# Block sums of w1 from DRAM scratch, and 512-column block products in three passes of a token-mixing MLP kernel

## The chip, the cores and the metric

The kernel runs on one NeuronCore of a Trainium2 chip. The core has TensorE (PE in the profile, with its weight loads listed apart as PEld), VectorE (DVE), ScalarE (ACT) and GpSimd (POOL), and SyncE (SP), which here only issues transfers. Sixteen DMA engines carry the transfers that SP, ACT and POOL issue. Each engine works through its own queue in order and waits on semaphores for the others. Matrix products accumulate in PSUM, which the kernel's pools divide into banks of 128 x 512 float32. The metric is the time of one execution on the device in microseconds (us), the median over the runs.

## The reference

One sequence of S = 2048 tokens with D = 512 channels, all float32. First an attention block with a learned feature map in 32 heads, then a token-mixing MLP with F = 1792 hidden units:

```python
qkv = _layernorm(x) @ wqkv                      # split into q, k, v, 32 heads of 16
phi = concat([softmax(q @ w_phi), softmax(-q @ w_phi)])      # the same for k
kv  = einsum("bhsf,bhsd->bhfd", phi_k, v);  z = phi_k summed over s
h   = x + (phi_q @ kv / (phi_q . z + 1e-6)) @ wo
n   = _layernorm(_layernorm(h))
u   = gelu(einsum("bsd,sf->bdf", n, w1) + b1)   # (512, 1792): tokens are contracted
y   = einsum("bdf,fs->bds", u, w2) + b2
out = h + y transposed
```

The change touches the first product of the MLP, `n` with `w1` (2048 x 1792). That is the reference's longest product together with the one with `w2`.

## The kernel before, in words

**Precision.** Every float32 operand is split into a high part of reduced precision (`hi`, made by a ScalarE copy) and the remainder (`lo`, made by a subtraction on VectorE or POOL). A product is three matmuls: hi x hi, hi x lo, lo x hi. `mm3` (lines 71 to 73) issues these; the third is the first that needs the lo part of its stationary operand. `split` (lines 66 and 67) makes the two parts.

**Stages.** The first stage (up to about 130 us) loads x in 16 tiles of 128 tokens, splits each (`split_x`: hi on ScalarE, lo on POOL) and computes k, v and q logits from it. `k_step(t)` multiplies tile t by the k weights, normalises the keys of tile t - 1 (`k_norm`, on VectorE and POOL), and loads and splits tile t + 2 into one of three raw buffers. The sums over tokens of keys and values (`kv`) are formed for four tiles at a time; the first four follow the v product of tile 4. In this stage the order of TensorE's work is written out by hand. The queues of SP, POOL, VectorE and ScalarE are there ordered by the framework's scheduler, which simulates the program and puts an instruction where it becomes ready, so the order in the queue need not be the order of the code. From the middle of the kernel on (from `ms`, after the last k product) all five orders are those of the code.

A second stage (up to about 263 us) forms the attention output and h. The MLP follows.

**The products with w1.** Seven passes, each over 256 columns of w1 (p = 0 to 6) and all 2048 tokens. Passes 0 and 1 run beside the second stage. The others are named by `KINDS = "vuuuv"`: pass 2 and pass 6 are plain ("v"), passes 3, 4 and 5 are block passes ("u"). A pass has eight steps of 256 tokens; steps are numbered through, so passes 3, 4, 5 are steps 8 to 31. After them come the products with w2 ("y" steps, from `Y0` = 40).

A block step takes a 256 x 256 piece of w1 as a 2 x 2 array of blocks and, instead of eight block products, forms seven, from sums of blocks of both operands. The seven weight blocks of a step lie in places 0 to 6 of a raw tile: 1 to 4 are the blocks of w1 as loaded, 0, 5 and 6 are sums, and place 1 is overwritten with a sum at the end. `w_sums` (lines 793 to 805) makes these on VectorE for a pair of steps. `w_parts` (808 on) splits a step's seven blocks into hi and lo. `load_raw(g)` issues the loads of pair g on SP, into one of four pair places (two tiles of two pairs); `prepare` calls it as soon as both steps of the pair that had the place are split.

**The seven products.** `products` (line 1007) issues each of them with `narrow` (line 989): three matmuls over 256 columns (hi x hi, hi x lo, lo x hi), 21 per step. The other form, `wide` (lines 996 and 998), takes hi x (hi and lo together) over 512 columns into a whole bank and then lo x hi over 256 columns into the bank's first half, so that two matmuls and two weight loads do the work of three; the bank's halves are added afterwards. The y steps (`wide_step`) have four of the seven products in this form and three as `narrow`: 17 matmuls per step. The block passes do not use it.

**Banks.** A block pass before uses four banks: pass 4 those of `ps_b`, passes 3 and 5 those of `ps_f` and `ps_q`. So two passes in a row use different banks. `u_out` (with `firsts`) forms the four output pieces from them: one ScalarE copy and five VectorE operations, issued right after the pass's last step has been issued.

**Adding transfers.** A DMA issued from POOL can add into its destination. The kernel has this in three places: for sums of u (line 951), for some weight sums of the y steps (line 790) and for the output (line 1039). SP's transfers cannot add. Each transfer that is issued on SP or ACT takes one of eight semaphores in turn (`DMAHW0` to `7` in the listings below), and waits for the transfer that had it before.

Of the kernel before, what the change touches and what calls it, by code (L numbers as in the profile page):

```python
# [9 lines left out]
F32 = mybir.dt.float32  # L10
# [7 lines left out]
P = 128  # L18
# [15 lines left out]
PLAIN = 2  # L34
KINDS = "vuuuv"
HD = D // 2
# [6 lines left out]
def block_kernel(ctx: ExitStack, tc: tile.TileContext, x, xT, wT, phic, wo, w1, b1, w2, b2,  # L43
# [61 lines left out]
    kvp = ps_kv.tile([P, 4, 64], F32, name="kvp")  # L105

# [174 lines left out]
    with tc.tile_pool(name="prep", bufs=1) as prep:  # L281
# [511 lines left out]
    def w_sums(g):  # L793
# [3 lines left out]
        plain = STEPS[2 * g][0] == "y"  # L797
        raw = BLOCK[g // 2 % 2] if plain else RAW[g]
# [8 lines left out]
    def w_parts(n):  # L807
# [8 lines left out]
        split(PARTS[n][0][:, k], PARTS[n][1][:, k], RAW[n // 2][:, n % 2, k], nc.vector)  # L816
# [189 lines left out]
    def four_banks(i):  # L1006
        return [new_bank(q) for q in ((ps_b,) * 4, (ps_f, ps_f, ps_q, ps_q))[i]]
# [7 lines left out]
    def firsts(banks):  # L1015
        a, b, c, d = banks
        tmp = wqp.tile([P, 4, HD], F32, name="tmp", tag="small")
        nc.scalar.activation(tmp[:, 1], a[:, 0], AF.Copy)
        nc.vector.tensor_sub(tmp[:, 2], a[:, 1], tmp[:, 1])
        nc.vector.tensor_sub(tmp[:, 3], tmp[:, 2], d[:, 0])  # L1020
        nc.vector.scalar_tensor_tensor(tmp[:, 0], b[:, 0], -1.0, tmp[:, 2], op0=ALU.mult, op1=ALU.subtract)
        return tmp[:, 0:2], tmp[:, 3].unsqueeze(1).to_broadcast([P, 2, HD])

    def u_out(p, banks):
        e, u3 = firsts(banks)
        U[p] = o = ur.tile([P, 4, HD], F32, name="u")
        nc.vector.tensor_add(o[:, 0:2], banks[1], u3)
        nc.vector.tensor_add(o[:, 2:4], banks[2], e)
# [187 lines left out]
    def prepare(m):  # L1216
# [8 lines left out]
        elif m % 2 == 0 and m + 2 < Y0:  # L1225
            w_sums(m // 2 + 1)
# [27 lines left out]
def _layout(A_x, A_wqkv, A_w_phi, A_wo, B_w1, B_b1, B_w2, B_b2):  # L1254
# [7 lines left out]
    for a in range(P // DH):  # L1262
# [11 lines left out]
        "w1": np.asarray(B_w1),  # L1274
        "b1": np.asarray(B_b1).reshape(NF, P).T,
# [23 lines left out]
```

## Time and profile before

| | |
|---|---|
| median of 3 runs | 515.43 us (515.14 to 515.83) |
| profiled execution, first to last instruction (span) | 513.1 us |
| outside the span, against the median | 2.3 us |
| granted TensorE clock | 1.000 |
| TensorE busy | 507.8 us (99%) |
| weight loads busy | 441.7 us (86%) |
| VectorE, ScalarE, POOL busy | 438.4 (85%), 310.6 (61%), 261.1 (51%) us |
| block passes (steps 8 to 31) | 288.6 to 349.1 us |
| y steps | from 370.9 us |

The page gives the profiled execution by its span; its own device time is not listed apart from the three runs, so it is held against their median here. A row of the page's groups names line, engine, operation, output and inputs; a row of a timeline begins with start and duration. A row of the chain has start, duration and what ran. In a row of the waits stand who waited, for whom, the total in us, how often, and the longest. In a row by windows, each engine's busy time stands with its number of instructions, and at the end the granted clock, the busy share of the DMA engines and GB/s. "To landing" is the time from issue to the transfer's completion. Matmuls overlap, so the duration of one (0.28 or 0.39 us) is longer than the distance to the next, which is what counts.

### The profile page before, as it was taken

Reading aid. Unit: us, or ns where it says so; the run is one execution under the profiler, and the core shown is the slowest. Engines: PE = TensorE matmul, PEld = TensorE weight load, DVE = VectorE, ACT = ScalarE, POOL = GpSimd, SP = SyncE. Lnnn points to the kernel's source line nnn. Section 1 sums busy time; section 2 is a strip of 40 time slices with the busy share of each in tenths; the row PEclk is TensorE's granted clock in tenths of the full one; section 3 lists DMA queues with packets and bytes.
Section 4 is the critical chain, followed back from the end, with each engine's and each line's share of the span. In section 5 each row is a group of like instructions: output and inputs, shape, how many; then the busy total and the mean of one; then the engine's idle time right before and its main releaser. Section 6 shows DMA issues by size and latency. Waiting matters only on the chain.

```text
span 513.1 us, 10496 instructions
## 1 busy us (share of the span) xinstructions
PE 507.8 (99%) x4024; PEld 441.7 (86%) x4024; DVE 438.4 (85%) x746; ACT 310.6 (61%) x557; POOL 261.1 (51%) x212
## 2 busy tenths in 40 slices
PE   8999999999999999999999999999999999999997
PEld 8888888888877777777788999998899999999997
DVE  6799889989887899699877898898799889868983
ACT  6999863525267878867676754577655444434530
POOL 3579997876999999985200421202323212211220
PEclk9999999999999999999999999999999999999999
DMA  8642301010123234354325775545677797668734
GB/s 308 217 144 84 103 22 42 1 65 21 42 64 103 67 100 145 127 169 132 95 69 185 150 159 125 133 115 151 173 164 147 181 199 167 122 153 190 169 51 85
DMA packets 53266, 63.35 MB, mean 123 GB/s; under 512 B 4832, under 2 KB 39904, under 8 KB 53216
## 3 DMA queue, kind: packets, MB, share of 16 engines
q1 hardware_dynamic: 44288, 51.90, 32.5%
q0 software_dynamic: 8640, 10.62, 14.9%
q8 instruction: 31, 0.51, 0.4%
q10 hardware_dynamic: 288, 0.17, 0.1%
q14 instruction: 19, 0.16, 0.1%
HBM read 48.39 MB, written 11.14 MB: 116 GB/s over the span
## 4 chain that ended last, share of the span: by engine, by line
PE 95%; DVE 2%; ACT 1%; DMA 1%; issue 0%; POOL 0%; DVEq 0%
PE py L989 25%; PE py L996 9%; PE pu L71 9%; PE pu L72 8%; PE pu L73 8%; PE py L998 4%; PE pk_ps L71 3%; PE pk_ps L72 3%; PE pk_ps L73 3%; PE pv L73 3%; PE pv L71 3%; PE pv L72 3%; PE po L71 3%; PE po L73 2%; PE po L72 2%; PE pn L616 2%
## 5 line engine op out<-in xcount | busy, mean ns | idle before, releaser
L66 ACT ACTIVATE wp<-wraw 128x896 fp32r<-128x896 f32 (+1 forms) x96 | 82.4, 895 | 68.3 <-DVE wraw L805 23.9
L67 DVE TENSOR_TENSOR wp<-wraw,wp 128x896 fp32r<-128x896 f32 (+1 forms) x96 | 95.5, 1019 | 14.9 <-ACT wp L66 14.6
L989 PE MATMUL py<-cb,wp 128*128 128x256 f32 x678 | 92.6, 283 | 0.0
L989 PEld LDWEIGHTS py<-cb,wp 128*128 128x128 f32 x678 | 86.1, 191 | 0.0
L1039 POOL DMA_DIRECT2D out<-u x28 | 24.8, 963 | 89.8 <-ACT u L1085 28.9
L951 POOL DMA_DIRECT2D tt<-u x14 | 13.4, 960 | 60.6 <-ACT tt L950 34.5
L490 POOL TENSOR_TENSOR ez<-eq,zB 128x1024 f32<-128x1024 f32 x16 | 38.4, 2406 | 3.8 <-ACT zB L550 3.8
L219 POOL TENSOR_TENSOR pk<-pk,sk 128x1024 f32<-128x1024 f32 x16 | 31.1, 1947 | 11.3 <-DVE sk L218 10.1
L996 PE MATMUL py<-cb,wp 128*128 128x512 f32 x126 | 36.1, 394 | 0.0
L514 POOL TENSOR_TENSOR eq<-eq,w 128x1024 f32<-128x1024 f32 x16 | 32.4, 2025 | 3.5 <-DVE w L511 3.5
L223 POOL TENSOR_TENSOR zacc<-zacc,pk 128x1024 f32<-128x1024 f32 x13 | 31.4, 2412 | 0.5
L989 PE MATMUL py<-hs,wp 128*128 128x256 f32 x216 | 30.0, 283 | 0.0
L989 PEld LDWEIGHTS py<-hs,wp 128*128 128x128 f32 x216 | 27.8, 192 | 0.1
L195 ACT ACTIVATE pk<-pk,r 128x1024 f32<-128x1024 f32 x16 | 18.4, 1149 | 15.0 <-DVE pk L173 14.4
L989 PE MATMUL py<-uf,wp 128*128 128x256 f32 x198 | 26.6, 283 | 0.0
L71 PE MATMUL pu<-wq,xs 128*128 128x512 f32 x64 | 26.1, 409 | 0.0
L71 PE MATMUL pu<-hs,whl 128*128 128x512 f32 x64 | 26.0, 406 | 0.0
L71 PE MATMUL po<-woh,oh 128*128 128x512 f32 x64 | 25.3, 396 | 0.1
L72 PE MATMUL pu<-wq,xs 128*128 128x512 f32 x64 | 25.0, 391 | 0.0
L73 PE MATMUL pu<-wq,xs 128*128 128x512 f32 x64 | 25.0, 390 | 0.0
L72 PE MATMUL pu<-hs,whl 128*128 128x512 f32 x64 | 25.0, 390 | 0.0
L73 PE MATMUL po<-woh,ol 128*128 128x512 f32 x64 | 25.0, 390 | 0.0
(226 smaller groups left out, 1422.1 us busy)
## 6 DMA issues: line engine op xcount, KB each, us to landing
wraw<-in_w SPq DMA_DIRECT2D x112, 256.0 KB, 3.4
out<-u POOLq DMA_DIRECT2D x21, 256.0 KB, 5.4
xraw<-in_xT SPq DMA_DIRECT2D x16, 256.0 KB, 2.9
xh<-in_x SPq DMA_DIRECT2D x16, 256.0 KB, 2.7
h<-in_x SPq DMA_DIRECT2D x16, 256.0 KB, 2.9
out<-h SPq DMA_DIRECT2D x16, 256.0 KB, 2.0
wraw<-in_wT SPq DMA_DIRECT2D x12, 256.0 KB, 4.9
tt<-u POOLq DMA_DIRECT2D x14, 128.0 KB, 3.8
```

The source lines that it names most:

```text
L66: nc.scalar.activation(hi, src, AF.Copy)
L67: lo_engine.tensor_sub(lo, src, hi)
L71: nc.tensor.matmul(o, ah, bh, start=first, stop=False)
L72: nc.tensor.matmul(o, ah, bl, start=False, stop=False)
L73: return nc.tensor.matmul(o, al, bh, start=False, stop=last).ins
L219: nc.gpsimd.tensor_mul(heads(PK[t]), heads(PK[t]), sk.unsqueeze(2).to_broadcast([P, 2 * H, DH]))
L223: nc.gpsimd.tensor_add(zacc, zacc, PK[t])
L490: nc.gpsimd.tensor_mul(EZ[t], EQ[t], zB)
L514: nc.gpsimd.tensor_mul(heads(EQ[t]), heads(EQ[t]), W[t].rearrange("p g c h -> p (g c h)").unsqueeze(2).to_broadcast([P, 2 * H, DH]))
L989: nc.tensor.matmul(o, w[:, m[0]], x[:, y], start=opens and i == 0, stop=closes and i == 2, skip_group_check=True)
L996: nc.tensor.matmul(o, wh_[:, m[0]], x(m[1]), start=first, stop=False, skip_group_check=True)
L1039: nc.gpsimd.dma_start(out[t * P:(t + 1) * P, k * HD:], flat(a), accum_op=ALU.add)
```

## The change

Two of the four weight sums of a block step are no longer made on VectorE. They come from DRAM scratch (`ZS`, two tensors of 512 KB for each block pass). These are filled in the first stage: `sum_copy` copies one set of w1's blocks from DRAM to DRAM on SP, and `sum_add` adds another set into it with an adding transfer on POOL. There are six of each. The code calls them in `k_step` from t = 5 and from t = 9. For this the host passes w1's columns of the block passes a second time, in the order of the blocks (`w1u`).

`load_raw` of a block pair loads blocks 2 to 4 from `w1u` in one transfer and the two sums from the scratch in two. The raw tile of a pair is laid out block by block, with the two steps side by side. `w_sums` is called for two pairs at once and makes the remaining two sums of both in two operations of 512 elements.

The products of a block step use `wide` for four of the seven. A block pass has six banks: four of `ps_b` in all three passes, and two of `ps_q` or `ps_f` in turn. `u_out` has five ScalarE copies and nine VectorE operations.

```diff
@@ in block_kernel
+    def sum_copy(p, k):
+        nc.sync.dma_start(rows(ZS[p][k]), rows(w1u[US.index(p), (2, 0)[k]]))
+
+    def sum_add(p, k):
+        nc.gpsimd.dma_start(rows(ZS[p][k]), rows(w1u[US.index(p), k]), accum_op=ALU.add, max_dma_last_dim=8192)
@@ in k_step
             k_norm(t - 1)
+            if 5 <= t < 11:
+                sum_copy(US[(t - 5) // 2], (t - 5) % 2)
+            if 9 <= t < 15:
+                sum_add(US[(t - 9) // 2], (t - 9) % 2)
@@ in load_raw
+        kind, i, j = STEPS[2 * g]
+        if kind == "u":
+            RAW[g] = RAW[g].rearrange("p n m s -> p (n m s)").rearrange("p (m n s) -> p m n s", m=7, n=2)
+            cols = slice(j * P, j * P + 2 * P)
+            nc.sync.dma_start(RAW[g][:, 2:5].rearrange("p m n s -> p m (n s)"),
+                              w1u[US.index(i), 1:4, :, cols].rearrange("m p s -> p m s"))
+            for k in range(2):
+                nc.sync.dma_start(RAW[g][:, k].rearrange("p n s -> p (n s)"), ZS[i][k][:, cols])
+            return
@@ in w_sums
-        plain = STEPS[2 * g][0] == "y"
-        raw = BLOCK[g // 2 % 2] if plain else RAW[g]
+        raw = BLOCK[g // 2 % 2]
+        if STEPS[2 * g][0] == "u":
+            v = raw.rearrange("p (g n) m s -> p g (n m s)", g=2).rearrange("p g (m s) -> p g m s", m=7)
+            nc.vector.tensor_add(v[:, :, 5], v[:, :, 0], v[:, :, 2])
+            nc.vector.tensor_add(v[:, :, 6], v[:, :, 4], v[:, :, 5])
+            return
@@ products
-        a, b, c, d = banks
-        for o, m, opens in ((a[:, 0], P1, True), (a[:, 1], P6, False), (d[:, 0], P7, True), (b[:, 0], P5, True),
-                            (b[:, 1], P4, False), (c[:, 0], P3, True), (c[:, 1], P2, False)):
-            narrow(o, n, m, x(m[1]), first and opens, last)
+        b16, b7, b5, b4, b3, b2 = banks
+
+        def singles():
+            narrow(b16[:, 0], n, P1, x(P1[1]), first, last)
+            narrow(b16[:, 1], n, P6, x(P6[1]), False, last)
+            narrow(b7[:, 0], n, P7, x(P7[1]), first, last)
+
+        w3, w2, w5, w4 = (b3, P3), (b2, P2), (b5, P5), (b4, P4)
+        if last:
+            singles()
+            wide(n, x, first, last, w5, w4)
+            wide(n, x, first, last, w3, w2)
+        elif first:
+            wide(n, x, first, last, w3, w2)
+            singles()
+            wide(n, x, first, last, w5, w4)
+        else:
+            wide(n, x, first, last, w3, w2, w5, w4)
+            singles()
@@ u_out (firsts is gone)
+        nc.scalar.activation(e1, b16[:, 0], AF.Copy)
+        for k, b in enumerate((b5, b4, b3, b2)):
+            nc.scalar.activation(o[:, k], b[:, 1], AF.Copy)
+        sub(u2, b16[:, 1], e1)
+        sub(u3, u2, b7[:, 0])
+        add(o[:, 0], b5[:, 0], o[:, 0])
+        add(o[:, 1], b4[:, 0], o[:, 1])
+        nc.vector.scalar_tensor_tensor(e0, o[:, 0], -1.0, u2, op0=ALU.mult, op1=ALU.subtract)
+        add(o[:, 0], o[:, 0], u3)
+        add(o[:, 2], b3[:, 0], o[:, 2])
+        add(o[:, 3], b2[:, 0], o[:, 3])
+        add(o[:, 1:4], o[:, 1:4], tmp[:, 0:3])
@@ in step
-                BANKS[0] = four_banks(i % 2)
+                BANKS[0] = six_banks((ps_f, ps_q)[i % 2])
@@ in prepare
-        elif m % 2 == 0 and m + 2 < Y0:
+        elif m % 4 == 2 and m + 2 < Y0:
             w_sums(m // 2 + 1)
```

How this stands in the queues. First POOL, early in the first stage. `xs` are the split x tiles (the second row is that of tile 2, the row that waits for `DMAHW7` that of tile 3), `r1` is a power for a tile's scale. Before:

```order
L67 TENSOR_TENSOR xs_226<-xraw_128,xs_226 128x512 [waits DMAHW6_49,Activation_49]
L67 TENSOR_TENSOR xs_302<-xraw_137,xs_302 128x512 [waits DMAHW4_49,Activation_49]
L133 TENSOR_TENSOR r1_67<-ve_316,mhalf_64 128x1 [waits DVE_49]
L67 TENSOR_TENSOR xs_340<-xraw_143,xs_340 128x512 [waits DMAHW7_49,Activation_49]
L133 TENSOR_TENSOR r1_67<-ve_347,mhalf_64 128x1 [waits DVE_49]
L67 TENSOR_TENSOR xs_351<-xraw_153,xs_351 128x512 [waits DMAHW0_49,Activation_49]
L67 TENSOR_TENSOR xs_525<-xraw_516,xs_525 128x512 [waits DMAHW2_49,Activation_49]
```

The same place after the change; `zs3_0` to `zs5_1` are the scratch tensors of passes 3 to 5, and these rows are the adding transfers:

```order
L68 TENSOR_TENSOR xs_310<-xraw_145,xs_310 128x512 [waits DMAHW4_49,Activation_49]
L118 DMA zs3_0_116<-in_w1u 64x2048 [waits DMAHW7_49]
L118 DMA zs3_1_117<-in_w1u 64x2048 [waits DMAHW1_49]
L146 TENSOR_TENSOR r1_67<-ve_324,mhalf_64 128x1 [waits DVE_49]
L118 DMA zs4_0_118<-in_w1u 64x2048 [waits DMAHW3_49]
L68 TENSOR_TENSOR xs_348<-xraw_151,xs_348 128x512 [waits DMAHW0_49,Activation_49]
L118 DMA zs4_1_119<-in_w1u 64x2048 [waits DMAHW4_49]
L146 TENSOR_TENSOR r1_67<-ve_355,mhalf_64 128x1 [waits DVE_49]
L68 TENSOR_TENSOR xs_359<-xraw_161,xs_359 128x512 [waits DMAHW2_49,Activation_49]
L68 TENSOR_TENSOR xs_533<-xraw_524,xs_533 128x512 [waits DMAHW6_49,Activation_49]
L118 DMA zs5_0_120<-in_w1u 64x2048 [waits DMAHW7_49]
```

Three adding transfers now stand between the lo part of tile 2 (`xs_310`) and that of tile 3 (`xs_348`), each with a wait for its copy.

Second SP, at the same time: the loads of x tiles 3 and 4 (`xraw`), of the rows of x for the statistics (`xh`) and, before them, of small constants. Before:

```order
L116 DMA xh_151<-in_x 128x512 [waits DMAHW3_49]
L308 DMA mask_62<-in_kvmask 128x64 [waits DMAHW4_49]
L309 DMA b1s_65<-in_b1 128x14 [waits DMAHW5_49]
L310 DMA b2s_66<-in_b2 128x16 [waits DMAHW6_49]
L111 DMA xraw_143<-in_xT 128x512 [waits DMAHW7_49,Pool_49]
L111 DMA xraw_153<-in_xT 128x512 [waits DMAHW0_49,Pool_49]
L116 DMA xh_155<-in_x 128x512 [waits DMAHW1_49,Activation_49]
```

After, with the copies into the scratch (16 rows of 8192 elements each):

```order
L129 DMA xh_159<-in_x 128x512 [waits DMAHW3_49]
L321 DMA mask_62<-in_kvmask 128x64 [waits DMAHW4_49]
L322 DMA b1s_65<-in_b1 128x14 [waits DMAHW5_49]
L323 DMA b2s_66<-in_b2 128x16 [waits DMAHW6_49]
L115 DMA zs3_0_116<-in_w1u 16x8192 [waits DMAHW7_49]
L124 DMA xraw_151<-in_xT 128x512 [waits DMAHW0_49,Pool_49]
L115 DMA zs3_1_117<-in_w1u 16x8192 [waits DMAHW1_49]
L124 DMA xraw_161<-in_xT 128x512 [waits DMAHW2_49,Pool_49]
L115 DMA zs4_0_118<-in_w1u 16x8192 [waits DMAHW3_49]
L115 DMA zs4_1_119<-in_w1u 16x8192 [waits DMAHW4_49]
L129 DMA xh_163<-in_x 128x512 [waits DMAHW5_49,Activation_49]
```

The copies take the places and the semaphores right behind the constants; the loads of tiles 3 and 4 each move behind one more copy.

Third TensorE, the second step of the first block pass (`hs` and `cb` hold the tokens and their block sums, `wp` the step's split weights, `py` the banks). Before:

```order
L989 MATMUL py_3703<-hs_2183,wp_3691 128x256 x3
L989 MATMUL py_3703<-cb1_3448,wp_3691 128x256 x3
L989 MATMUL py_3706<-cb1_3448,wp_3691 128x256 x3
L989 MATMUL py_3704<-cb1_3448,wp_3691 128x256 x6
L989 MATMUL py_3705<-hs_2283,wp_3691 128x256 x6
```

After:

```order
L1027 MATMUL py_3722<-hs_2303,wp_3709 128x512
L1027 MATMUL py_3723<-hs_2303,wp_3709 128x512
L1027 MATMUL py_3726<-cb1_3468,wp_3709 128x512
L1027 MATMUL py_3727<-cb1_3468,wp_3709 128x512
L1029 MATMUL py_3722<-hs_2303,wp_3709 128x256
L1029 MATMUL py_3723<-hs_2303,wp_3709 128x256
L1029 MATMUL py_3726<-cb1_3468,wp_3709 128x256
L1029 MATMUL py_3727<-cb1_3468,wp_3709 128x256
L1020 MATMUL py_3724<-hs_2203,wp_3709 128x256 x3
L1020 MATMUL py_3724<-cb1_3468,wp_3709 128x256 x3
L1020 MATMUL py_3725<-cb1_3468,wp_3709 128x256 x3
```

The step has 17 matmuls in place of 21, four of them over 512 columns, and six banks in place of four.

More of the change, by code (lines that the diff above doesn't have):

```diff
@@ L35 @@
 KINDS = "vuuuv"
+US = [p for p, k in enumerate(KINDS, PLAIN) if k == "u"]
 HD = D // 2
@@ L42, in block_kernel @@
 @with_exitstack
-def block_kernel(ctx: ExitStack, tc: tile.TileContext, x, xT, wT, phic, wo, w1, b1, w2, b2,
+def block_kernel(ctx: ExitStack, tc: tile.TileContext, x, xT, wT, phic, wo, w1, w1u, b1, w2, b2,
                  kvmask, ident_in, out):
@@ L105, in block_kernel, with rows @@
     kvp = ps_kv.tile([P, 4, 64], F32, name="kvp")
+    dram = ctx.enter_context(tc.tile_pool(name="dram", bufs=1, space=bass.MemoryType.DRAM))
+    ZS = {p: [dram.tile([P, NT // 2 * P], F32, name=f"zs{p}_{k}") for k in range(2)] for p in US}
+    def rows(a):
+        return a.rearrange("(a b) s -> a (b s)", b=2)
+    def sum_copy(p, k):
+        nc.sync.dma_start(rows(ZS[p][k]), rows(w1u[US.index(p), (2, 0)[k]]))
+    def sum_add(p, k):
+        nc.gpsimd.dma_start(rows(ZS[p][k]), rows(w1u[US.index(p), k]), accum_op=ALU.add, max_dma_last_dim=8192)
     X, XH, EQ, PK, VS, SQ, PS, W = {}, {}, {}, {}, {}, {}, {}, {}
@@ L1004, in new_bank, with six_banks @@
         return pool.tile([P, 2, HD], F32, name="py", tag="pu")
-    def four_banks(i):
-        return [new_bank(q) for q in ((ps_b,) * 4, (ps_f, ps_f, ps_q, ps_q))[i]]
+    def six_banks(pool):
+        b3, b2 = [new_bank(pool) for _ in range(2)]
+        return [new_bank(ps_b) for _ in range(4)] + [b3, b2]
     def products(n, banks, x, first, last):
-        a, b, c, d = banks
-        for o, m, opens in ((a[:, 0], P1, True), (a[:, 1], P6, False), (d[:, 0], P7, True), (b[:, 0], P5, True),
-                            (b[:, 1], P4, False), (c[:, 0], P3, True), (c[:, 1], P2, False)):
-            narrow(o, n, m, x(m[1]), first and opens, last)
@@ new lines, in u_out @@
+    def u_out(p, banks):
+        b16, b7, b5, b4, b3, b2 = banks
+        tmp = wqp.tile([P, 4, HD], F32, name="tmp", tag="small")
+        u3, e0, e1, u2 = [tmp[:, k] for k in range(4)]
+        U[p] = o = ur.tile([P, 4, HD], F32, name="u")
+        add, sub = nc.vector.tensor_add, nc.vector.tensor_sub
+        nc.scalar.activation(e1, b16[:, 0], AF.Copy)
[10 more added lines that the diff above has]
+        add(o[:, 1:4], o[:, 1:4], tmp[:, 0:3])
@@ L1274, in _layout @@
         "w1": np.asarray(B_w1),
+        "w1u": np.stack([np.asarray(B_w1)[:, 2 * P * p:2 * P * (p + 1)].reshape(NT // 2, 2, P, 2, P)
+                         .transpose(1, 3, 2, 0, 4).reshape(4, P, NT // 2 * P) for p in US]),
         "b1": np.asarray(B_b1).reshape(NF, P).T,
```

14 lines of the change are left out of this document (2 added, 12 removed).

## The prediction

> **What bounds the kernel now.** I read the page's busy times and slices first, then the table of waits of TensorE, then the chain of work that ended last, and last the queues of the first 50 us, because the change puts work there.
>
> ```profile
> PE 507.8 (99%) x4024; PEld 441.7 (86%) x4024; DVE 438.4 (85%) x746; ACT 310.6 (61%) x557; POOL 261.1 (51%) x212
> ...
> POOL 3579997876999999985200421202323212211220
> ...
> DMA  8642301010123234354325775545677797668734
> ...
> PE 95%; DVE 2%; ACT 1%; DMA 1%; issue 0%; POOL 0%; DVEq 0%
> ```
> TensorE is busy for 99% and makes up 95% of the chain. POOL is at 51% on average, but from the fourth slice (12.8 us each) to the eighteenth it is at six tenths and more, and the DMA engines are fullest in the first three slices. The next rows are all the waits that TensorE has:
>
> ```profile
> PE pk_ps L357 <- DVE eps L62: 1.1, 1, 1.1
> PE pu L335 <- POOL ph L361: 0.4, 1, 0.4
> PE pn L616 <- DVE h L641: 0.2, 1, 0.2
> ```
> So there is nothing to win but TensorE's own time, and whatever makes TensorE wait is added to the end in full: no later wait is there to absorb it.
>
> **What the wide form is worth.** The three u passes stand in the chain as one block of narrow products. The first y steps already multiply in the new form, two or four products at a time over 512 columns:
>
> ```profile
> 288.63 60.47 PE py L989 x504
> 349.11 0.23 PE pu L71
> ...
> 373.35 0.92 PE py L996 x4
> 374.27 0.47 PE py L998 x4
> 374.75 1.08 PE py L989 x9
> 375.82 0.93 PE py L996 x4
> ...
> 383.25 0.93 PE py L996 x4
> ```
> 504 matmuls in 60.47 us are 0.120 us each, and a step of 21 takes 60.47/24 = 2.520 us. A y step of 4 wide, 4 low and 9 narrow matmuls covers the same columns in (383.25 - 373.35)/4 = 2.475 us. The difference, 0.045 us, over 24 steps is **-1.07 us**. First and last steps of a pass hold the same 17 matmuls in another order, so I take the same price for them.
>
> The Trainium skill (TensorE: Matmul & The Clock Gate, Back-to-back issue gap) gives a matmul its columns at 2.4 GHz plus about 2.5 ns; by it the four matmuls saved per step would be worth 10 ns and the passes 0.24 us, so the sum would end 0.83 us higher. The rows disagree: 0.120 us for 256 columns is 13 ns above 107 ns, and the measurement decides.
>
> **VectorE and ScalarE in the u passes.** A pair of steps has four sums of 256 elements now, and two pairs will share two sums of 512. The closing sums grow from five VectorE operations to nine and from one ScalarE copy to five.
>
> ```profile
> 311.98 0.42 DVE L801 TENSOR_TENSOR wraw<-wraw 128x256 f32<-128x256 f32 x1
> ...
> 347.46 0.36 ACT L1018 ACTIVATE tmp<-py 128x256 f32<-128x256 f32 x1
> ...
> 347.73 0.68 DVE L67 TENSOR_TENSOR wp<-wraw,wp 128x512 fp32r<-128x512 f32 x1
> 348.33 0.42 DVE L1019 TENSOR_TENSOR tmp<-py,tmp 128x256 f32<-128x256 f32 x1
> 348.85 0.42 DVE L1020 TENSOR_TENSOR tmp<-tmp,py 128x256 f32<-128x256 f32 x1
> 349.19 0.42 DVE L1021 SCALAR_TENSOR_TENSOR tmp<-py,tmp 128x256 f32<-128x256 f32 x1
> 349.52 0.68 DVE L1027 TENSOR_TENSOR u<-py,tmp 128x512 f32<-128x512 f32 x1
> ```
> Per two pairs 8 x 0.42 becomes 2 x 0.68 us, 2.0 us less of VectorE; per pass end the sums rise by four VectorE operations (some 1.6 us) and four copies of 0.36 us. TensorE waits for neither today, so the relief is worth 0. The extra matters only through the banks: all three u passes now accumulate in the same four banks, so the next pass may not open b16 before `u2` is formed. Its counterpart (L1019) ends at 348.75 and TensorE leaves the pass at 349.11. In the tightest place, where the v pass takes that bank at once, that leaves 0.36 us; where a u pass follows, its first six matmuls (0.7 us) go to other banks. I cost this at 0; its cover is that 0.36 us.
>
> **Loads in the u passes.** A pair needs three SP transfers (640 KB) instead of two (512 KB). Pair g+1 is now summed two steps earlier, three steps (7.4 us) after its load is called for. The row on contention below has 2.9 us median and 4.8 us at most for a landing in these passes, so this is hidden: 0.
>
> **The scratch.** The scheduler puts the six copies on SP's queue right behind the last small constant, not at the fifth x tile where the code writes them, and the six adding transfers on POOL's queue from there on, each with a wait for its copy. POOL runs its queue in order, so what stands behind an add waits too. Third in line is the lo part of x tile 3, behind the adds of copies 1, 2 and 3.
>
> ```profile
> 15.02 1.28 POOL L67 TENSOR_TENSOR xs<-xraw,xs 128x512 fp32r<-128x512 f32 x1 [3.33 <-ACT xs L66]
> 17.62 0.56 POOL L133 TENSOR_TENSOR r<-ve,mhalf 128x1 f32<-128x1 f32 x1 [1.31 <-DVE ve L132]
> 18.96 1.30 POOL L67 TENSOR_TENSOR xs<-xraw,xs 128x512 fp32r<-128x512 f32 x1 [0.78 <-ACT xs L66]
> ...
> 22.45 0.39 PE L73 MATMUL pk_ps<-wkh,xs 128*128 128x512 f32 x1
> ```
> The third row is that lo part: it ends at 20.26, and TensorE's first use of it (the third matmul of the k product of tile 3) starts at 22.45. The slack is 2.2 us. Now for when copy 3 lands:
>
> ```profile
> 10.67 0.33 SPq L116 DMA_DIRECT2D xh<-in_x  x1
> 13.31 0.33 SPq L111 DMA_DIRECT2D xraw<-in_xT  x1
> 13.91 0.33 SPq L111 DMA_DIRECT2D xraw<-in_xT  x1
> ...
> xh<-in_x SPq DMA_DIRECT2D x1, 256.0 KB, 5.1
> xraw<-in_xT SPq DMA_DIRECT2D x1, 256.0 KB, 3.4
> ...
> 13.00:16.00 3.00, 3.00 (x21) 2.64 (x20) 2.74 (x5) 2.94 (x8) 0.98 (x1) 1.00 1.08 382
> ```
> Copy 1 takes the issue of 13.31. Copy 3 reuses the semaphore of the xh load of 10.67, so it issues at 10.67 + 5.1 = 15.8. Up to 16 us the DMA engines are full (share 1.08, 382 GB/s), so data move in turn. The two x loads landed at 13.31 + 3.4 = 16.7 and 13.91 + 3.4 = 17.3: 0.6 us per 256 KB. In the new order, with 512 KB a copy: copy 1 at 17.3, x tile 3 at 17.9, copy 2 at 19.1, x tile 4 at 19.7, copy 3 at 20.9. By then add 1 (issued at about 18.2) is also moving. How an adding transfer slows a plain one is seen in the u passes (first row) and beside stores that add (the other two, at 395 and 417 us):
>
> ```profile
> DMA to landing us min/median/max: 2.6/2.9/4.8
> ...
> DMA to landing us min/median/max: 4.1/4.1/4.1
> ...
> DMA to landing us min/median/max: 5.7/5.7/5.7
> ...
> L1039 POOL DMA_DIRECT2D out<-u x28: 862/865/1242, 390.2 to 504.0; - x28
> ```
> That is 1.2 to 2.8 us more. So copy 3 lands between 20.9 (untouched) and 23.7; I take 22.7, nearest to those two rows, since adds and copies are certain to overlap. Then add 3 is issued (0.87, the last row) and the lo part made (1.30): it ends at 22.7 + 2.2 = 24.9, and TensorE waits 24.9 - 22.45 = **+2.4 us**, between 0.6 and 3.4. No row shows a DRAM-to-DRAM copy or add; a copy that reads and writes DRAM at half the rate would put copy 3 near 24.5 and the wait near 4.3, the far end.
>
> The rest of the early work I cost at 0. The lo part of tile 4 needs 2.7 us of POOL after that of tile 3 (add 4 at 0.87, a power at 0.56, itself at 1.30) and up to some 2 us more if copy 4 is late; TensorE wants it 27.89 - 22.45 = 5.4 us after tile 3's (first row below). The six issues take 6 x 0.87 = 5.2 us of POOL, and POOL has 6.5 us idle there:
>
> ```profile
> 27.89 0.39 PE L73 MATMUL pk_ps<-wkh,xs 128*128 128x512 f32 x1
> ...
> 16.30:42.80 26.50, 26.50 (x136) 22.59 (x135) 23.84 (x42) 25.91 (x57) 20.00 (x18) 1.00 0.43 135
> ...
> 42.81 1.94 POOL L219 TENSOR_TENSOR pk<-pk,sk 128x1024 f32<-128x1024 f32 x1
> ...
> 47.45 1.99 PE L231 MATMUL kvp<-pk,vs 128*32 128x64 f32 x128
> ```
> The next hard date is the kv sums: tile 3's normalised keys end at 44.75 and are used in the last quarter of 47.45 to 49.4, about 48.9 (plus the 2.4 by which TensorE is late itself).
>
> **Sum.** -1.07 + 2.4 = +1.3 us. The profiled execution spans 513.1 us; the median of the runs is 515.43, 2.3 us more for what lies outside the span, which the change leaves alone. I predict 515.43 + 1.3 = **516.8 us**, 0.26% slower.
>
> **Rivals.**
> - *The copies are early, no wait.* Copy 3 must land by 22.45 - 2.2 = 20.25. Against it: 20.9 by the bytes queued ahead. For it: that 0.6 us is a rate for loads into SBUF, and the queue may drain otherwise. Then only the wide form counts: 514.4. The Trainium skill (DMA: Bandwidth & Descriptors, Anatomy of one DMA — SWDGE (gpsimd) path) prices one transfer at about 2.0 us plus its bytes at 436 GB/s, an estimate of 3.2 us for a copy; copy 3 issued at 15.8 would land at 19.0, and this rival would hold. The rows have 5.1 us for 256 KB in this stretch, since others stand ahead.
> - *The copies queue, but the adds hardly disturb them.* Copy 3 at 20.9 to 21.7: the wait is 0.6 to 1.5 us and cancels the gain, 515.4.
> - *POOL does not catch up.* Copies 5 and 6 queue behind four adds; if their waits hold POOL for 9 us beyond its idle time, tile 3's keys come at 44.75 + 9 = 53.8 and TensorE, there at 48.9 + 2.4 = 51.3, waits another 2.5 us: 519.3. For it: POOL's slices read 9, 9, 9 from 38 to 77 us. Against it: 6.5 us idle ahead.
> - *The banks.* If VectorE comes 1 us late at the pass ends, up to three waits of 0.7 us are added: 518.9. Against it: the relief of 2.0 us per two pairs.
>
> **How the numbers follow.** About 0.2%, 1.0 us, is what a measurement of this kernel tells from no change. Forecast 0.49 (its own range 516.2 to 517.8), weak disturbance 0.26, early copies 0.12, POOL late 0.08, banks 0.05. Faster is the early case, 0.12; same is the weak one, 0.26; slower is the rest, 0.62. The range reaches from the early case (514.3) to the late POOL (519.6), which also holds the half-rate copy.
>
> **What would show it.** Right: the u passes in one piece of 24 x 2.475 = 59.4 us without waits; in the waits a new row of TensorE on POOL in the k product of tile 3, near 22.5 us, for 1.8 to 3.4 us, and a POOL wait for an SP copy ahead of the add. Wrong: no such row (early copies), a second one at the kv sums, or waits for VectorE at 308, 328 or 348 us. A u step that is not near 2.475 us would break the first term.

## The result, and the profile after

The changed kernel takes 530.81 us (median of 6 runs, 528.33 to 537.28), the kernel before 515.63 us beside it: a ratio of 1.0295, 95% interval 1.0276 to 1.0315. The slowest of the six (537.28 us) ran in a slower state and is not in the ratio; without it the median is 530.66 us. It is 15 us slower where 1.3 us was predicted. The profiled execution spans 529.2 us, 16.1 us more than before.

First the page of the kernel after: busy time, the granted clock and DMA by slices (13.2 us each), and the chain that ended last.

```profile
PE 513.3 (97%) x3928; PEld 440.0 (83%) x3928; DVE 433.4 (82%) x722; ACT 314.4 (59%) x569; POOL 265.7 (50%) x218
...
PEclk9989899999999999999999999999999999999999
DMA  8997430102012234345226495636586887687843
...
PE 71%; DVE 11%; DMA 8%; issue 5%; ACT 4%; POOL 0%; SPq 0%; DVEq 0%; POOLq 0%; ACTq 0%
```

The second and third slice of the DMA engines read 9 where they read 6 and 4 before. The chain has left TensorE for 8% DMA and 11% VectorE, and the clock is below full in two early slices. Next the kernel after's waits of TensorE; two short rows that stood before as well are left out.

```profile
PE pk_ps L74 <- POOL xs L68: 3.1, 1, 3.1
PE pv L72 <- ACT vs L223: 2.3, 1, 2.3
PE pu L348 <- DVE wq L366: 2.2, 2, 1.9
PE pu L348 <- DVE wraw L340: 1.4, 1, 1.4
...
PE py L1020 <- DVE u L1129: 0.8, 1, 0.8
PE py L1020 <- DVE tmp L1071: 0.8, 1, 0.8
PE pk_ps L72 <- DVE pk L186: 0.5, 1, 0.5
```

The first row is the wait that was predicted. The next three, and the last, are in the first 55 us too and were not. The two `py` rows are in the y steps (L1129) and between two block passes (L1071). To see how much time each stage lost, here is TensorE's timeline of the kernel after at the first kv sums, the first block step and the first matmul behind the block passes.

```profile
62.47 1.75 PE L244 MATMUL kvp<-pk,vs 128*32 128x64 f32 x109
...
303.42 0.62 PE L1027 MATMUL py<-hs,wp 128*128 128x512 f32 x2
...
363.78 0.45 PE L72 MATMUL pu<-hs,wp 128*128 128x512 f32 x1
```

Before, these three stood at 47.45 (a row of the prediction), 288.47 and 348.94 us:

```profile
288.47 0.52 PE L989 MATMUL py<-hs,wp 128*128 128x256 f32 x3
...
348.94 0.40 PE L71 MATMUL pu<-hs,wp 128*128 128x512 f32 x1
```

So 15.0 us are lost before the first kv sums, nothing between there and the block passes (240.95 against 241.02 us), 0.1 us is won in the block passes (60.36 against 60.47), and the y steps take 1.3 us more (139.28 against 138.02). Why the first stage is late, the chain of the kernel after says in one row; behind it, the waits of the other engines between 8 and 62 us.

```profile
18.39 17.87 DMA xraw<-in_xT
```

```profile
POOL xs L68 <- ACT xs L67: 15.1, 4, 8.2
DVE ve L145 <- ACT sqj L143: 14.7, 2, 14.2
ACT xs L67 <- DMA xraw<-in_xT: 11.4, 1, 11.4
```

The load of x tile 5 (256 KB) took 17.9 us; before, no x load took over 5.0 us. These are the landings of the x tiles in the first 65 us, before and after:

```profile
DMA to landing us min/median/max: 2.6/3.4/5.0
```

```profile
DMA to landing us min/median/max: 2.7/4.4/17.9
```

ScalarE has the split of that tile in its queue at 24.9 us and waits 11.4 us for it. VectorE waits 14.2 us for a statistic that stands behind it on ScalarE, and POOL 8.2 us for the high part of the tile. TensorE had work until 35.9 us; from there to 54.3 us it runs out five times, 6.45 us in all, because keys, values and the folded q weights come late.

There is one more loss in this stage, in the granted clock (the column after the instruction count).

```profile
26.00:27.00 1.00, 0.70 (x3) 1.00 1.05 217
27.00:28.00 1.00, 1.00 (x5) 0.56 0.95 186
...
30.00:31.00 1.00, 1.00 (x5) 0.73 1.04 231
```

After the 3.1 us wait TensorE runs at half clock for 3.4 us, which costs 1.7 us (the missing parts of 27 to 31 us added up). The same comes back from 54 to 58 us, another 1.7. The 15.0 us are then 9.5 us of waits, 3.4 us of clock, 0.6 us by which TensorE was late at 15 us already, and 1.5 us that I can't place.

### The profile page after: what moved, and what is told of

Same layout as the page of the kernel before. It is cut to its first block, busy times and chain, and to the rows that moved or that the text cites. A ratio compares the mean times of both kernels' runs of the same rounds, so it can differ in the third digit from the quotient of the medians.

```text
span 529.2 us, 10326 instructions
## 1 busy us (share of the span) xinstructions
PE 513.3 (97%) x3928; PEld 440.0 (83%) x3928; DVE 433.4 (82%) x722; ACT 314.4 (59%) x569; POOL 265.7 (50%) x218
## 4 chain that ended last, share of the span: by engine, by line
PE 71%; DVE 11%; DMA 8%; issue 5%; ACT 4%; POOL 0%; SPq 0%; DVEq 0%; POOLq 0%; ACTq 0%
PE py L1020 12%; PE pu L72 8%; PE py L1027 7%; PE pu L73 7%; PE pu L74 7%; PE py L1029 4%; DMA xraw<-in_xT 3%; DMA wraw<-in_w 3%; DVE wp L68 3%; PE po L72 3%; PE po L74 2%; PE po L73 2%; PE pv L74 2%; PE pv L72 2%; PE pv L73 2%
## 5 line engine op out<-in xcount | busy, mean ns | idle before, releaser
L67 ACT ACTIVATE wp<-wraw 128x896 fp32r<-128x896 f32 (+1 forms) x96 | 82.4, 895 | 65.9 <-DVE wraw L835 24.5
L1020 PE MATMUL py<-cb,wp 128*128 128x256 f32 x534 | 75.3, 283 | 0.8 <-DVE u L1129 0.8
L1020 PEld LDWEIGHTS py<-cb,wp 128*128 128x128 f32 x534 | 68.7, 190 | 1.0 <-DVE u L1129 1.0
L1027 PE MATMUL py<-cb,wp 128*128 128x512 f32 x174 | 51.3, 395 | 0.0
L982 POOL DMA_DIRECT2D tt<-u x14 | 13.3, 949 | 60.7 <-ACT tt L981 47.7
L1027 PEld LDWEIGHTS py<-cb,wp 128*128 128x128 f32 x174 | 29.7, 189 | 3.8
L1029 PEld LDWEIGHTS py<-cb,wp 128*128 128x128 f32 x174 | 28.5, 188 | 4.1
L1029 PE MATMUL py<-cb,wp 128*128 128x256 f32 x174 | 31.0, 279 | 0.0
L74 PE MATMUL pk_ps<-wkh,xs 128*128 128x512 f32 x60 | 24.4, 407 | 3.1 <-POOL xs L68 3.1
L68 POOL TENSOR_TENSOR xs<-xraw,xs 128x512 fp32r<-128x512 f32 x15 | 19.6, 1323 | 15.1 <-ACT xs L67 15.1
L72 PE MATMUL pu<-wq,xs 128*128 128x512 f32 x64 | 26.1, 408 | 0.0
L72 PE MATMUL pv<-wvh,xs 128*128 128x512 f32 x60 | 23.7, 395 | 2.3 <-ACT vs L223 2.3
L72 PE MATMUL pu<-hs,whl 128*128 128x512 f32 x64 | 25.9, 405 | 0.0
```

The lines of the kernel that those rows point to most:

```text
L67: nc.scalar.activation(hi, src, AF.Copy)
L68: lo_engine.tensor_sub(lo, src, hi)
L72: nc.tensor.matmul(o, ah, bh, start=first, stop=False)
L74: return nc.tensor.matmul(o, al, bh, start=False, stop=last).ins
L1020: nc.tensor.matmul(o, w[:, m[0]], x[:, y], start=opens and i == 0, stop=closes and i == 2, skip_group_check=True)
L1027: nc.tensor.matmul(o, wh_[:, m[0]], x(m[1]), start=first, stop=False, skip_group_check=True)
```

## The experiments

Theory A, formed from this profile: the twelve transfers fill the DMA engines from 14 to 47 us, so that tile 5 is late. Theory B is the prediction's: the waits of the adding transfers in POOL's queue. Theory C: the new form or loads of the block passes. The table has all runs; "x load" is the slowest landing of an x tile in the first 65 us, "first kv" the start of the first kv sums, "u" and "y" the lengths of block passes and y steps, all in us from the profiled execution. The ratio is to the kernel before on the same chip, whose median over the three groups of runs was 515.3 to 515.6.

| run | median us | ratio (95%) | x load | first kv | u | y |
|---|---|---|---|---|---|---|
| before | 515.4 | | 5.0 | 47.4 | 60.47 | 138.02 |
| after | 530.81 | 1.0295 (1.0276 to 1.0315) | 17.9 | 62.5 | 60.36 | 139.28 |
| e1_scratch_only | 529.37 | 1.0266 (1.0249 to 1.0283) | 17.0 | 61.6 | 60.48 | 139.77 |
| e2_late | 520.07 | 1.0088 (1.0065 to 1.0111) | 4.9 | 48.3 | 60.42 | 138.56 |
| e3_copies_only | 517.37 | 1.0056 (1.0032 to 1.0079) | 8.1 | 49.2 | 60.16 | 138.82 |
| e4_half_early | 524.31 | 1.0175 (1.0131 to 1.0220) | 9.9 | 53.6 | 61.40 | 138.02 |
| e5_wide_alone | 516.08 | 1.0016 (1.0007 to 1.0024) | 5.2 | 47.5 | 61.24 | 138.02 |
| e6_lo_on_vector | 528.49 | 1.0252 (1.0237 to 1.0267) | 17.3 | 59.8 | 61.44 | 138.03 |
| e7_mid | 518.08 | 1.0061 (1.0036 to 1.0085) | 5.1 | 47.5 | 64.32 | 138.39 |
| e8_mid_banks | 515.39 | 1.0003 (0.9990 to 1.0015) | 4.8 | 48.0 | 59.32 | 138.05 |
| e9_no_accum | 521.00 | 1.0104 (1.0084 to 1.0124) | 11.3 | 55.0 | 60.38 | 138.02 |
| e10_four_two | 514.65 | 0.9991 (0.9981 to 1.0002) | 5.5 | 47.7 | 59.32 | 138.47 |
| e11_wide_order | 515.40 | 1.0005 (0.9996 to 1.0014) | 5.0 | 47.5 | 60.83 | 138.04 |

**The scratch alone.** The kernel before, with the change's two helpers, its scratch and this addition:

```diff
             k_norm(t - 1)
+            if 5 <= t < 11:
+                sum_copy(US[(t - 5) // 2], (t - 5) % 2)
+            if 9 <= t < 15:
+                sum_add(US[(t - 9) // 2], (t - 9) % 2)
```

> The kernel before with the six copies and six adding transfers of the change added at the same calls, and nothing reading the sums; loads, VectorE sums and narrow form as before. Theory A (the scratch's 12 transfers fill the DMA engines from 14 to 47 us, so the load of x tile 5 lands 17.9 us after its call, and ScalarE, VectorE and TensorE stand behind it): nearly the whole loss comes with the scratch, 515.5 + 15.1 = 530.6 us (528 to 533), first block of kv sums at about 62.5 us. Theory B (my prediction's: only the waits of the adding transfers on GpSimd, ahead of the low part of x tile 3, cost time, 3.1 us, and the half clock after it 1.7 us): 515.5 + 4.8 = 520.3 us. Theory C (the loss comes from the new form or the new loads of the u passes): 515.5 us.

529.37 us: 13.8 of the 15.2 us come with the scratch, though nothing reads it, and tile 5's load takes 17.0 us again. Theory C falls. The first wait was 2.9 us here; B's 4.8 us in all don't cover the loss.

**POOL's queue freed.** Theory B's wait is taken away with the transfers left as they were:

```diff
-            split(X[t][:, 0], X[t][:, 1], raw, nc.gpsimd)
+            split(X[t][:, 0], X[t][:, 1], raw, nc.vector if 3 <= t <= 5 else nc.gpsimd)
```

> The changed kernel with the low parts of x tiles 3, 4 and 5 made on VectorE instead of GpSimd, so that no adding transfer stands ahead of them; all 12 transfers stay in their order on SyncE and GpSimd. Theory A: the bytes are the same, tile 5's load still lands 15 to 18 us after its call; only the first wait (3.1 us and the 1.7 us of half clock after it) can go: 524 to 530 us. Theory B: the loss of the first stage goes but for VectorE's three extra operations of 0.7 us: 515.5 to 518 us.

528.49 us. The wait at tile 3 is gone, and the waits of this run between 8 and 62 us show what stands in its place:

```profile
DVE xs L68 <- ACT xs L67: 12.7, 2, 9.8
ACT xs L67 <- DMA xraw<-in_xT: 10.5, 1, 10.5
...
PE pk_ps L72 <- DVE ve L145: 9.6, 1, 9.6
```

TensorE waits once, for 9.6 us, at the end of a line that begins with the same load (17.3 us). Theory B falls as the main cause: with the load of tile 5 as late as it is, taking POOL's order away gains 2.3 of 15 us (2.7 us at the first kv sums).

**Copies without adds, and adds that don't add.** In the first run the calls of `sum_add` are left out; in the second the transfers stay, and overwrite:

```diff
     def sum_add(p, k):
-        nc.gpsimd.dma_start(rows(ZS[p][k]), rows(w1u[US.index(p), k]), accum_op=ALU.add, max_dma_last_dim=8192)
+        nc.gpsimd.dma_start(rows(ZS[p][k]), rows(w1u[US.index(p), k]), max_dma_last_dim=8192)
```

> The changed kernel without the six adding transfers (the two sums then hold one block each instead of two); the six copies stay where they were. Theory A with the adding transfers as the heavy part (the DMA rate falls from 380 to 220 GB/s while they run): the copies alone are 3.15 MB, 8 us at 380 GB/s, so the load of tile 5 lands 8 to 10 us after its call, at 27 to 28 us, ScalarE waits 2 to 3 us and TensorE little: 515 to 518 us. If the copies alone hold the queue (16 pieces of 32 KB each ahead of the load): load of tile 5 still over 14 us, 525 to 530 us. Theory B: no wait on GpSimd is left, 515.7 us.

> The changed kernel with the six adding transfers turned into plain transfers onto the same scratch (same bytes, same place on GpSimd, same waits for their copies; the sums then hold one block each). If the read and write of an adding transfer is what fills the DMA engines (217 to 230 GB/s in the stretches where they run, 373 GB/s where copies run alone): 3.15 MB at 380 GB/s are 8 us instead of 14, tile 5's load lands about 10 us earlier than in the changed kernel, and the total is 517 to 522 us. If it is the bytes and the second queue, whatever the transfer does: 526 to 531 us. Theory B: the waits on GpSimd stay, 520 us.

Without adds 517.37 us, as theory A had it, with tile 5 at 8.1 us. With plain transfers in their place 521.0 us, within what was expected, but that doesn't decide between A (517 to 522) and B (520). Tile 5 came 6.6 us earlier, not 10, and in this run TensorE never waits for it. Its only wait from 8 to 62 us is theory B's:

```profile
PE pk_ps L74 <- POOL xs L68: 4.2, 1, 4.2
```

From 27 to 33 us, behind this wait, the granted clock is 0.50, which costs 3.0 us. Together these are 7.2 of the 7.5 us by which the first kv sums are late here. So with plain transfers the wait that I predicted, and the half clock behind it, are nearly the whole loss of the stage; with adding transfers the late load of tile 5 makes the loss twice as large, and taking POOL's order away then gains only the 2.3 us of e6. Here is what the transfers cost the 16 DMA engines, by queue from 13 to 47 us: packets, MB, and share of the engines' time. First the kernel after, then the run that overwrites.

```profile
q1 hardware_dynamic: 2449, 6.52, 53.6%
q0 software_dynamic: 471, 3.14, 47.1%
```

```profile
q0 software_dynamic: 480, 3.15, 24.0%
```

For the same 3.15 MB the adding transfers hold all engines for 0.471 x 34 = 16.0 us, plain ones for 8.2 us. Adding doubles the price of a byte, and the two queues together fill the 34 us to 100%. The Trainium skill (DMA: Bandwidth & Descriptors, Issuing engines are not separate DMA queues) states that transfers of all issuing engines run on the same 16 DMA engines and interleave. The rows agree: POOL's transfers delay SP's load.

**Half the bytes early.** Each copy and add is cut in two by rows; the second halves follow at about 111 us (copies) and 122 to 132 us (adds).

```diff
-    def sum_add(p, k):
-        nc.gpsimd.dma_start(rows(ZS[p][k]), rows(w1u[US.index(p), k]), accum_op=ALU.add, max_dma_last_dim=8192)
+    def sum_add(p, k, h=0):
+        a = slice(32 * h, 32 * h + 32)
+        nc.gpsimd.dma_start(rows(ZS[p][k])[a], rows(w1u[US.index(p), k])[a], accum_op=ALU.add, max_dma_last_dim=8192)
```

> The changed kernel with every copy and adding transfer cut in two by rows: the first half (256 KB) at the place of the change, the second half behind the loads of wo and at 122 to 132 us; sums complete, 12 transfers early as before but with half the bytes. The loss before the first kv sums was 15.1 us with all bytes (62.5 against 47.4 us). Theory A (time on the DMA engines): half the bytes are some 10 us of engine time less ahead of the load of tile 5; it lands about 9 us earlier, at 27 us, where ScalarE wants it at 25, and most of the loss goes: first kv sums at 48 to 52 us, total 516 to 521 us. If the count of transfers or their waits on each other make the loss: first kv sums at 57 us or later, total over 524 us.

524.31 us, outside A's range and just inside that of the other reading (over 524); the first kv sums start at 53.6 us, between A's 48 to 52 and the other reading's 57. A left out a wait in the block passes (1.77 us in this profile, see below) and was too hopeful for the stage. The single times go from 520.99 to 527.65 us, and the profiled run took 522.65. Half the bytes leave 6.2 of 15.1 us, and tile 5's load falls from 17.9 to 9.9 us. So the bytes set most of the loss: half of them leave 41% of it, though all twelve early transfers and their waits on each other are still there.

**Where the scratch costs nothing.** Three placements, all with the copies behind the loads of `wo` (about 111 us) instead of in `k_step`. In e2 the adds go one to a turn of the second stage, from turn 12; in e7 they stand as in this diff; in e10 the last two are in turns 11 and 12 instead.

```diff
         nc.sync.dma_start(WO[j], wo[j * P:(j + 1) * P, :])
+    for i in range(6):
+        sum_copy(US[i // 2], i % 2)
...
+    for i in range(4):
+        sum_add(US[i // 2], i % 2)
     s_ez(0)
...
+    for i in range(4, 6):
+        sum_add(US[i // 2], i % 2)
     s_pq(0)
```

> The changed kernel with the six copies called behind the loads of wo (about 111 us) and the six adding transfers one per turn of the second stage from turn 12 on (about 225 to 262 us); all else as changed. Theories A and B: the first stage is as in the kernel before (first kv sums at 47.5 us, not 62.5), so 530.8 - 15.1 = 515.7 us; with the two 0.8 us waits of TensorE on VectorE in the u and y passes gone as well 514.2 us, with them kept 515.7. Theory C: 528 to 531 us. If the adding transfers cost GpSimd's stage time anywhere they are put, 517 to 520 us.

The first stage recovers (first kv sums at 48.3 us), but 520.07 us is 4 us above what A made of it. The adds collide with the loads of the second stage. Here are the transfers called from 225 to 270 us in this run (count, KB each, median us to landing), and then the loads of h in the kernel before.

```profile
zs<-in_w1u POOLq DMA_DIRECT2D x6, 512.0 KB, 5.9
...
out<-h SPq DMA_DIRECT2D x6, 256.0 KB, 5.3
h<-in_x SPq DMA_DIRECT2D x4, 256.0 KB, 6.1
```

```profile
h<-in_x SPq DMA_DIRECT2D x4, 256.0 KB, 2.9
```

The loads of h take twice as long. TensorE's waits come through other loads of that stage, those of weights (`wraw<-in_w`): from 225 to 262 us they took 5.7 us in the median, against 3.9 before, and ScalarE, which splits them, waited for them for 8.6 us from 230 to 290 us, against 2.2 before.

```profile
ACT whl L692 <- DMA wraw<-in_w: 8.6, 5, 3.0
```

VectorE stands behind this split, and TensorE waits 0.91, 0.29 and 1.75 us for VectorE at 252, 259 and 266 us.

> The changed kernel with the copies behind the loads of wo (about 111 us) and the adding transfers on GpSimd ahead of its first products with the reciprocal sums (four ahead of the first, two behind the second, about 122 to 132 us), where the DMA engines of the kernel before moved 2 to 47 GB/s. Theory A: no load waits there, so neither the 15.1 us of the first stage nor the 3 us that the late placement showed in the turns at 252 to 266 us; what is left is the wide form's -0.9 us and a wait on a bank of about 0.8 us: 515.4 us (514.5 to 516.5). If adding transfers cost what their issue takes on GpSimd (six times 0.87 us) wherever they are: 518 to 521 us.

Here the adds run where the DMA engines of the kernel before were nearly idle (2 to 47 GB/s). The first stage is whole (47.5 us), and up to the block passes TensorE has only the waits that it has in the kernel before. Yet the run takes 518.08 us, with single times from 515.9 to 521.9. The rest is in the block passes: 64.32 us in the profiled run, with 2.9 us of waits and 1.7 us of half clock. The single times go with the granted clock: 519.8 us and more in the four runs where it was 0.997 or less, 518.5 and less in the six where it was 0.999 or 1.000.

**The banks.** TensorE's wait between two block passes came in the kernel after, in e2, e3, e4, e6, e7 and e9, with 0.6 to 2.2 us each. What it waits for is VectorE's read of bank b16, which waits for ScalarE's copy of that bank (`tmp<-py`). ScalarE's timeline in e7, and behind it TensorE's:

```profile
310.81 0.42 ACT L983 ACTIVATE tt<-tt 128x256 f32<-128x256 f32 x1 [3.09 <-DMA tt<-u]
311.13 0.36 ACT L1070 ACTIVATE tmp<-py 128x256 f32<-128x256 f32 x1
```

```profile
312.01 0.62 PE L1022 MATMUL py<-hs,wp 128*128 128x256 f32 x3 [2.17 <-DVE tmp L1073]
```

ScalarE stands for 3.09 us before a scaling that belongs to the block sums of an earlier result and waits for an adding transfer. The copy that frees the bank is next in line. Before, the passes took turns in different banks, and a late copy held up nobody. The next run moves the last of those scalings (and its transfer) one step later, behind the copy:

```diff
-    U_ADDS = {0: (5, 7, 9), 1: (6, 8, 10), 2: (11, 13, 15), 3: (19, 21, 23), 4: (28, 30, 32), 5: (34, 35.5, 37)}
+    U_ADDS = {0: (5, 7, 9), 1: (6, 8, 10), 2: (11, 13, 16), 3: (19, 21, 24), 4: (28, 30, 32), 5: (34, 35.5, 37)}
```

> As the run before with copies at 111 us and adding transfers at 122 to 132 us, and in addition the third piece of the block sums of u pass results 2 and 3 (a scaling on ScalarE that waits for an adding transfer) one step later, so that it no longer stands on ScalarE ahead of the copies that free the banks b16, b7, b5 and b4 for the next pass. If the 0.6 to 0.9 us waits of TensorE at the first products of the second and third u pass come from that order: they go, u passes 59.6 us, total 0.8 us below the run before, about 514.6 us. If VectorE's own chain of sums ahead of the bank is what is waited for: as the run before.

ScalarE's timeline in that run, at the same pass end:

```profile
308.05 0.36 ACT L1070 ACTIVATE tmp<-py 128x256 f32<-128x256 f32 x1
...
310.91 0.42 ACT L983 ACTIVATE tt<-tt 128x256 f32<-128x256 f32 x1
```

The copy comes first, the passes have no wait and take 59.32 us, and the total is 515.39 us: 2.7 us below e7, not the expected 0.8, because in e7 the waits were longer than in the runs from which the 0.8 was taken, and half clock came behind them.

**Two more versions.** One asks whether POOL's lateness cost the 0.6 us that e8 still lost between the first kv sums and the block passes; the others do without the scratch.

> The kernel with copies at 111 us, adding transfers at 122 to 132 us and the third pieces one step later, with the last two adding transfers moved to the ends of turns 11 and 12 of the second stage (about 222 to 232 us), so that GpSimd is not 1.2 us later from 133 us on. That kernel took 241.6 us from the first kv sums to the first u step, the kernel before 241.1. If the lateness of GpSimd is what costs that 0.6 us: 515.4 - 0.6 = 514.8 us, 0.1% below the kernel before. If two adding transfers among the loads of the second stage cost as six did there (4.5 us for six): 516 to 517 us.

> The wide form, its six banks and the new combination of a pass's results alone: no scratch, w1 loaded in blocks and all four sums made on VectorE as in the kernel before. Theory A (the loss is the scratch's transfers): first stage as before, first kv sums at 47.5 us. Of the u passes: the traces with the wide form show 60.2 to 61.4 us from the first to the last of their steps with waits of TensorE of 0.56 to 1.56 us in them (59.6 to 59.9 us without), before 60.5 us; VectorE does 0.7 us more per step here. If VectorE holds: 515.5 - 0.9 + 0.8 (one wait on a bank) = 515.4 us. If VectorE, with 0.36 us of margin before, falls behind: each of the 24 steps up to 0.3 us, 517 to 521 us.

> The kernel with the wide form alone (no scratch, sums on VectorE), with the third pieces of the block sums of u pass results 2 and 3 one step later. Its trace showed u passes of 61.24 us with waits of TensorE of 0.2 (on VectorE's low parts) and 0.87 us (leaving the last pass, on VectorE's combination). If the order on ScalarE was behind the bank waits there too: 515.3 us. If VectorE is the bound with the sums made on it: as the wide form alone, 516.1 us.

e10 has 241.0 us there, as before, and takes 514.65 us, as expected. Its interval overlaps with that of e8, so the gain over e8 is not shown by the times. Its block passes in the windows view, in one piece:

```profile
288.69:348.01 59.32, 59.32 (x409) 55.13 (x408) 50.12 (x69) 40.83 (x67) 14.34 (x17) 1.00 0.63 163
```

The median is 0.7 us below that of the kernel before, of the 1.07 us that the wide form was forecast to bring. With an interval of 0.9981 to 1.0002 this can't be told from no change, so no version here is shown to beat the kernel before. With the sums on VectorE (e5) the wide form gains nothing: 61.24 us, 60.83 with the scalings moved (e11). In both, 0.85 us is a wait when TensorE leaves the last pass; the other 0.7 to 1.1 us against 59.32 is left open. On these runs the wide form shortens the passes only together with the scratch.

## Why the prediction was wrong, step by step

*The wide form, -1.07 us.* Right. Where nothing waits, the passes take 59.32 us, 2.472 us a step: -1.15 us. The 0.24 us that the prediction worked out from the Trainium skill (TensorE: Matmul & The Clock Gate, Back-to-back issue gap) came from its figure for an isolated matmul; the section itself says that a stream of matmuls with a weight load each is spaced otherwise, at 128 columns further apart. The block passes are such a stream (120 ns for 256 columns), so the rows do not contradict it. In the kernel after, 0.76 us of the gain went to the bank wait, and 0.3 us I can't place.

*VectorE and ScalarE in the block passes, 0.* Wrong by 0.76 us here and up to 2.9 in e7. The cover was named rightly (the four banks that all passes now share, 0.36 us of margin) and the place too, but I looked for a late VectorE. It was ScalarE's queue, with a wait for a DMA ahead of the copy that frees the bank. The rival *banks* had 0.05.

*Loads in the block passes, 0.* Right: no wait for them in e8 and e10.

*The wait at the k product of tile 3, +2.4 us.* Right in place and mechanism, 3.1 us in size, inside 0.6 to 3.4. That it stayed inside was luck: POOL's wait for copy 3 ended at 24.1 us, later than the 20.9 to 23.7 worked out for it and near the half-rate case (24.5), but TensorE came 0.8 us later too (23.2 against 22.45 us). The 1.7 us of half clock behind it were not in the sum.

*"The rest of the early work I cost at 0."* This is the step that failed, with some 10 us (15.0 less 3.1 and 1.7). I followed what stands in POOL's queue, and counted POOL's own time for the issues (5.2 against 6.5 us idle). The time of the transfers on the DMA engines was not added up, and the loads that share them (tile 5 and after) were not asked about. In the runs the DMA engines are full from 13 to 47 us, the load of tile 5 takes 17.9 us where none took over 5.0, and with the transfers elsewhere (e7) the first kv sums stand at 47.5 us again. The page of the kernel before had the prices, in its queues over the whole span:

```profile
q1 hardware_dynamic: 44288, 51.90, 32.5%
q0 software_dynamic: 8640, 10.62, 14.9%
```

Plain transfers take 0.325 x 513.1 / 51.90 = 3.2 us of all engines per MB, adding ones 0.149 x 513.1 / 10.62 = 7.2. From 14 to 47 us, 33 us, the engines were 46% busy (the second number from the end), 15 us:

```profile
14.00:47.00 33.00, 33.00 (x172) 28.15 (x171) 30.08 (x53) 32.31 (x70) 25.48 (x20) 1.00 0.46 143
```

Six copies add 3.15 x 3.2 = 10 us, six adds 3.15 x 7.2 = 23 us. That is 48 us of transfers for 33 us. With the price measured since (5.1 us per MB) it is 41.

*Rivals.* *Early copies* and *weak disturbance* took the DMA engines to be free soon, and the estimate from the Trainium skill (DMA: Bandwidth & Descriptors, Anatomy of one DMA — SWDGE (gpsimd) path), 3.2 us for a copy, met a median of 8.1 us to landing for the six copies. That fit is for transfers that GpSimd issues, one by one; the copies are SP's and had others beside them. *POOL does not catch up* named lateness in the same stage, but blamed the waits of the adds; without them e6 gains 2.3 us. With plain transfers (e9) these waits and the half clock behind them are nearly all of the loss.

*Not the change's.* Of the 1.3 us in the y steps, 0.76 us is a wait for VectorE at L1129. It was 1.29 us in e1, whose block passes are those of before, and absent in others; y took 138.0 to 139.8 us over the runs. Its cause wasn't tried.

## What to carry to other kernels

Before moving transfers into a stage, add up the DMA engines' time there: the share they have already, plus the bytes at each queue's own price from the profile's page, adding transfers apart from plain ones. If the sum exceeds the stage, the victims are the loads with the next due date, however little the issuing engine has to do. And where buffers or banks stop alternating, read the queue of every engine that frees them up to the freeing instruction: a wait of something unrelated ahead of it becomes yours.

## What the runs showed of the hardware

An adding transfer from DRAM to DRAM costs twice a plain one of the same shape: 16.0 against 8.2 us of all DMA engines for 3.15 MB. In the stretches where they ran, the kernel after moved 186 to 231 GB/s with the engines full (24 to 31 us), against 373 GB/s from 15 to 20 us.

The clock fell to half after idle times of different length, and not after each. In e7 2.17 us were enough; from there on:

```profile
312.00:313.00 1.00, 0.99 (x7) 0.86 0.37 127
313.00:314.00 1.00, 1.00 (x6) 0.50 0.84 131
...
316.00:317.00 1.00, 1.00 (x8) 0.94 0.06 16
```

In the kernel after 3.08 us led to it, and so did 1.85 us (to 54.30 us); 2.34 us (to 38.25 us) did not. The half clock lasted 3.4 us both times there and in e7, and cost 1.7 us each time. In e9 it lasted 6.8 us (26.2 to 33.0 us) and cost 3.0. The changes of the clock stand at 27.1, 30.5, 54.4 and 57.8 us in the kernel after: 1, 7 and 1 times 3.41 us apart; the two in e9 are 2 times that apart, the two in e6 (30.7 and 40.9 us) 3 times. This would fit idle time that is counted in fixed stretches of 3.41 us: the 1.85 us lie whole in one of them, the 2.34 us across the border of two (1.46 and 0.88 us). No run was made to test it. The Trainium skill (TensorE: Matmul & The Clock Gate, Part 1: The HAM clock gate) gives about 3.4 us for an idle window and for the way back; the way back agrees in the kernel after and in e7 and took twice that in e9, and the idle time that sufficed here was shorter.
